# Second MLP's first weights decoded one unit per tile through a single buffer, and the token sums and splits moved from GpSimd to VectorE and spaced out

## The chip, the core and the metric

The kernel runs on one NeuronCore of a Trainium2 chip. TensorE (PE; its weight loads are shown as PEld), VectorE (DVE), ScalarE (ACT), GpSimd (POOL) and SyncE (SP, which here only issues DMAs) each work through a queue of their own in order, and wait for each other by semaphores. The metric is device time in microseconds, as a median over runs.

## What is computed

```python
def _moe_ref(x, w_in, w_out):            # first MLP
    h = x @ w_in
    g = h * (1.0 / (1.0 + np.exp(-1.702 * h)))
    return (g @ w_out).astype(np.float32)

def _moe2_ref(x, w_in, w_out):           # second MLP
    h = x @ w_in
    g = h * np.cos(h)
    return (g @ w_out).astype(np.float32)

# reference: attention of x (8 batches, 8 heads, 512 tokens, width 64) against 32 states,
# and of the states against x, gives 8 * (512 + 32) = 4608 rows of width 512;
# then _moe_ref and _moe2_ref over these rows (d_ff 2048), in float32
```

## The kernel before

Every float32 operand is split into a high part that TensorE takes exactly and a low rest, and a product is three matmuls (high-high, high-low, low-high). Weights come from HBM as 64-bit words of which a *unit* of 1024 columns is put together on chip: `top` and `bottom` on ScalarE, `bits` on VectorE, then `hi` (a copy on ScalarE) and `lo` (a subtraction on VectorE).

**First MLP.** Its steps are (t, c): token tile t (512 tokens; the tail, t = 8, has 256 rows of the states) and chunk c of 16 of the hidden width. The order of the tiles is 0 to 6, then the tail, then 7. In a step TensorE makes `hidden` (the tile `ph`) and then `second` of the step two before (into `py`). ScalarE and VectorE make the gate between them: `t` (ACT), `t` (DVE), `gh` (ACT), `gl` (DVE). For t = 1 to 7 the attention's values are folded into the weights: `sw_piece` makes them (POOL issues their store to DRAM, `sd<-swo`), and `load_sw` brings them back, 256 KB a step (`swt`), into a ring of eight tiles: that of step c + 8 is issued by SP at step c.

**The second MLP's weights on the way.** The second MLP multiplies 2x2 blocks with seven products where eight would be plain. For that each unit of its first weights becomes eight *leaves*: four blocks and four sums. `leaves` decodes a unit, splits the blocks (`hi(0)`, `lo`), makes four sums in place (`sums`), splits these (`hi(1)` on ACT, the subtraction on POOL), and stores both halves to DRAM (`ld<-leaf`, 1 MB each). All eight units are fetched and decoded in the steps of the tail and of tile 7, in the buffers of the first MLP's input weights as these come free. In tile 7 `prepare_first` also makes the seven sums and splits of the first pair of token tiles, with POOL for the arithmetic and ACT for the high parts.

**Second MLP.** A list of work is put in order by `Order`, a planner with a cost and a due time for each piece, that writes out one fixed order for each engine. A pair of token tiles has eight periods; a period is 15 blocks of six matmuls: seven products (`bankX`, `bankY`, `bankW`) and eight blocks of the second weights (`bankpy`, `bankF`). The first period has the seven products and the first MLP's last two `second` pieces. In periods 1 to 8 `unit` decodes the eight units of the second weights. `prepare` makes the sums and splits of the next pair of tokens: raw tiles loaded by SP (`raw<-yd`), sums and low parts on POOL, high parts on ACT, stores to DRAM (`od`). Its due times lie 8 us apart, but a piece may start as soon as its operands are there.

The planner's rule for the next piece, of those that could start first:

```python
at = {n: begin(n) for n in some}
first = min(at.values()) + 0.05
n = min((n for n in some if at[n] <= first), key=lambda n: (work[n][4], n))
```

Of the kernel before, what the change touches and what calls it, by code (L numbers as in the profile page):

```python
# [10 lines left out]
F32 = mybir.dt.float32  # L11
# [32 lines left out]
GROUP = 15 * BLOCK  # L44


class Order:
# [9 lines left out]
    def add(self, engine, cost, do, reads=(), writes=(), due=0.0, lag=0.0):  # L57
# [11 lines left out]
        self.work.append((engine, cost, do, tuple(after), due, lag))  # L69

    def write(self):
# [15 lines left out]
        def begin(n):  # L87
            return max(free[work[n][0]], max((ends[a] + SIGNAL for a in work[n][3]), default=0.0))

        while len(begun) < len(work):  # L90
# [11 lines left out]
            e, cost, _, _, _, lag = work[n]  # L102
# [15 lines left out]
def attention_two_mlps(  # L118
# [17 lines left out]
    xp = ctx.enter_context(tc.tile_pool(name="xp", bufs=2))  # L136
    ep = ctx.enter_context(tc.tile_pool(name="ep", bufs=2))
# [30 lines left out]
    def fetch_w(m, nm, j):  # L168

        src = {"i": (w_in1, w_in2), "o": (w_out1, w_out2)}[nm][m]  # L170
        place = 2 * j % (KF // 2) if m and nm == "i" else j
        raw = wp.tile([P, UNIT, 2], I32, name=f"raw{nm}{m}_{j}", tag=f"w{nm}{place}")
        for e in range(2):
            words = src[2 * j + e].bitcast(I32)
            if m and nm == "i":
                nc.sync.dma_start(
                    out=raw.rearrange("p (h e k f) w -> p h e k (f w)", h=2, e=2, k=2)[:, :, e, :, :],
                    in_=words.rearrange("p (h k f) -> p h k f", h=2, k=2),
                )
            elif nm == "i":  # L180
# [30 lines left out]
    def decode_end(entry=None):  # L211
# [3 lines left out]
        if entry is None and begun[0][0] == 1 and begun[0][1] == "i":  # L215
            return leaves()
# [19 lines left out]
    late = []  # L236

    def leaves():

        _, _, j, u, low = begun.pop(0)  # L240
        place = 2 * j % (KF // 2)
        ui = u.bitcast(I32)
        uq = u.rearrange("p (q f) -> p q f", q=4)
        out_ = []

        def bits():
            nc.vector.scalar_tensor_tensor(  # L247
                out=ui, in0=ui, scalar=3, in1=low, op0=ALU.logical_shift_left, op1=ALU.bitwise_or
            )

        def hi(n):
            out_.append(wp.tile([P, 4, 2, PAIR], F32R, name=f"leaf{j}_{n}", tag=f"wi{place + n}"))
            nc.scalar.activation(out=out_[n][:, :, 0, :], in_=uq, func=AF.Copy)

        def lo(n, engine):
# [12 lines left out]
        def lo_and_sums():  # L268
            lo(0, nc.vector)
            sums()  # L270
            late.append(lambda: (hi(1), lo(1, nc.gpsimd)))

        return bits, lambda: hi(0), lo_and_sums


# [905 lines left out]
```

## Time and profile before

| | us |
|---|---|
| median of 3 runs (1478.27 to 1480.67) | 1479.16 |
| the profiled execution | 1481.61 |
| its span, first to last instruction | 1479.8 |
| TensorE busy in the span | 1418.8 |
| VectorE busy | 961.4 |
| ScalarE busy | 735.1 |
| GpSimd busy | 228.2 |

The profiled execution is 2.45 us longer than the median of the runs, and 1.8 us of it lie outside the span. A matmul of 128x512 starts 0.227 us after the one before when nothing is waited for, so six of them, a block, take 1.36 us at the full clock. The granted clock is a share of 2.4 GHz: 1.00 is 2.4 GHz, and a stretch wholly at 0.50 is at 1.2 GHz.

### The profile page before, as it was taken

What the parts mean: (1) busy time and instruction counts of PE and PEld (TensorE: products, weight loads), DVE (VectorE), ACT (ScalarE), POOL (GpSimd) and SP (SyncE); (2) the same over time, 40 slices, a digit from 0 to 9 for tenths busy, and PEclk for the clock granted to TensorE, in tenths of its full rate; (3) what the DMA queues carried; (4) which work ended last, traced back from release to release, by engine and by line L of the source; (5) the groups of instructions that cost most, each with busy time, mean ns of one, the idle gap of its engine ahead of it and who ended that gap; (6) DMA issues with size and microseconds to landing.
All of it is one profiled execution on the core that took longest, in us unless ns stands there. A gap on an engine that the chain in (4) does not pass through costs nothing.

```text
span 1479.8 us, 19839 instructions
## 1 busy us (share of the span) xinstructions
PE 1418.8 (96%) x7134; PEld 1161.5 (78%) x7134; DVE 961.4 (65%) x1589; ACT 735.1 (50%) x1253; POOL 228.2 (15%) x222
## 2 busy tenths in 40 slices
PE   8999999999999999967889999899989999999998
PEld 5878888888878788956767787788878888888887
DVE  6875646565556555557568867766677677666664
ACT  6764343434443434445477545544455444544454
POOL 1111111101110001015625002500053000000000
PEclk9999999999999999978989999999999999999999
DMA  9756564656464443669677527853398236423253
GB/s 345 223 175 186 160 184 142 193 139 174 132 183 121 136 125 86 226 235 388 238 230 239 185 86 284 300 184 93 119 345 282 94 92 233 151 86 93 88 176 107
DMA packets 128226, 268.58 MB, mean 181 GB/s; under 512 B 17280, under 2 KB 35328, under 8 KB 126080
## 3 DMA queue, kind: packets, MB, share of 16 engines
q1 hardware_dynamic: 119024, 237.81, 48.5%
q0 software_dynamic: 8960, 29.37, 8.0%
q8 instruction: 57, 0.93, 0.3%
q14 instruction: 41, 0.34, 0.1%
q10 hardware_dynamic: 144, 0.13, 0.0%
HBM read 181.27 MB, written 85.98 MB: 181 GB/s over the span
## 4 chain that ended last, share of the span: by engine, by line
PE 82%; DVE 8%; DMA 4%; ACT 3%; issue 2%; POOL 1%; SPq 0%; ACTq 0%; DVEq 0%; POOLq 0%
PE py L540 22%; PE bankpy L704 12%; PE bankF L704 11%; PE bankX L694 10%; PE ph L485 10%; PE bankY L694 5%; PE psS L300 3%; PE bankW L694 3%; PE ph L493 2%; PE psA L359 1%; DMA rawi<-in_w_in 1%; DVE u L247 1%; DMA ws<-ld 1%; DVE r L676 1%; DVE leaf L256 1%
## 5 line engine op out<-in xcount | busy, mean ns | idle before, releaser
L540 PE MATMUL py<-gh,wo 128*128 128x512 f32 (+1 forms) x1152 | 369.4, 384 | 9.6 <-ACT gh L500 6.3
L540 PEld LDWEIGHTS py<-gh,wo 128*128 128x128 f32 x1152 | 217.7, 193 | 54.1 <-ACT gh L500 6.5
L704 PE MATMUL bankpy<-wo,g 128*128 128x512 f32 x864 | 221.6, 392 | 4.5 <-DVE g L684 3.3
L540 PE MATMUL py<-gl,wo 128*128 128x512 f32 (+1 forms) x576 | 221.3, 384 | 1.9 <-DVE gl L502 1.9
L500 ACT ACTIVATE gh<-t 128x512 fp32r<-128x512 f32 (+1 forms) x144 | 87.5, 608 | 262.0 <-DVE t L512 132.7
L502 DVE TENSOR_TENSOR gl<-t,gh 128x512 fp32r<-128x512 f32 (+1 forms) x144 | 104.1, 723 | 163.4 <-ACT gh L500 163.4
L704 PE MATMUL bankF<-wo,g 128*128 128x512 f32 x768 | 200.0, 395 | 9.8 <-DVE acc L844 6.5
L704 PEld LDWEIGHTS bankpy<-wo,g 128*128 128x128 f32 x864 | 162.0, 189 | 39.6 <-DVE g L684 4.7
L485 PE MATMUL ph<-xh,swt 128*128 128x512 f32 x448 | 163.6, 406 | 16.5 <-DVE t L512 16.5
L704 PEld LDWEIGHTS bankF<-wo,g 128*128 128x128 f32 x768 | 145.1, 190 | 43.5 <-DVE acc L844 7.4
L512 DVE SCALAR_TENSOR_TENSOR t<-t,ph 128x512 f32<-128x512 f32 (+1 forms) x144 | 94.0, 653 | 88.3 <-ACT t L510 88.0
L308 POOL DMA_DIRECT2D sd<-swo x112 | 66.9, 607 | 499.2 <-DVE swo L305 475.9
L844 DVE SCALAR_TENSOR_TENSOR acc<-bankF,acc 128x512 f32<-128x512 f32 x112 | 77.3, 690 | 98.4 <-PE bankF L704 94.3
L672 ACT ACTIVATE r<-C 128x512 f32<-128x512 f32 (+1 forms) x144 | 87.1, 605 | 96.1 <-DVE C L893 95.3
L540 PEld LDWEIGHTS py<-gl,wo 128*128 128x128 f32 x576 | 111.0, 193 | 23.9 <-DVE gl L502 3.4
L485 PEld LDWEIGHTS ph<-xh,swt 128*128 128x128 f32 x448 | 85.4, 191 | 46.3 <-DVE t L512 18.2
L510 ACT ACTIVATE t<-ph 128x512 f32<-128x512 f32 (+1 forms) x144 | 81.8, 568 | 74.3 <-PE ph L485 61.7
L678 ACT ACTIVATE r<-r 128x512 f32<-128x512 f32 (+1 forms) x144 | 84.6, 603 | 61.6 <-DVE r L676 61.4
L676 DVE TENSOR_TENSOR r<-r,n 128x512 f32<-128x512 f32 (+1 forms) x144 | 107.4, 760 | 2.7
L684 DVE TENSOR_TENSOR g<-r,g 128x512 fp32r<-128x512 f32 (+1 forms) x144 | 94.8, 688 | 22.1 <-ACT g L682 21.4
L887 ACT ACTIVATE C<-bankX 128x512 f32<-128x512 f32 x96 | 57.1, 595 | 102.7 <-PE bankX L694 102.5
L680 DVE TENSOR_TENSOR r<-r,C 128x512 f32<-128x512 f32 (+1 forms) x144 | 96.8, 701 | 10.4 <-ACT r L678 10.1
(147 smaller groups left out, 2151.0 us busy)
## 6 DMA issues: line engine op xcount, KB each, us to landing
ws<-ld SPq DMA_DIRECT2D x256, 256.0 KB, 2.9
sd<-swo POOLq DMA_DIRECT2D x112, 256.0 KB, 3.9
swt<-sd SPq DMA_DIRECT2D x112, 256.0 KB, 4.1
rawi<-in_w_in SPq DMA_DIRECT2D x32, 512.0 KB, 7.6
rawo<-in_w_out SPq DMA_DIRECT2D x32, 512.0 KB, 7.2
ld<-leaf SPq DMA_DIRECT2D x16, 1024.0 KB, 4.9
xT_t<-in_xT SPq DMA_DIRECT2D x36, 256.0 KB, 4.3
xN_t<-in_xN SPq DMA_DIRECT2D x16, 512.0 KB, 4.4
```

Source lines behind the costliest of these rows:

```text
L485: nc.tensor.matmul(ph, l, r, start=(g == 0 and i == 0), stop=(g == 1 and i == 2))
L500: nc.scalar.activation(out=gh, in_=g, func=AF.Copy)
L502: return lambda: nc.vector.tensor_tensor(out=gl, in0=g, in1=gh.bitcast(F32), op=ALU.subtract)
L512: nc.vector.scalar_tensor_tensor(out=g, in0=t1, scalar=1.0, in1=ph, op0=ALU.add, op1=ALU.mult)
L540: nc.tensor.matmul(yt[k], l, r, start=(c == 0 and i == 0), stop=(c == KF - 1 and i == 2))
L672: add("ACT", 0.62 * u, lambda: nc.scalar.activation(out=R(), in_=C(), func=AF.Copy, bias=0.25), [ck], [rk], due - 5)
L676: add("DVE", 0.69 * u, lambda: nc.vector.tensor_tensor(out=R(), in0=R(), in1=N(), op=ALU.subtract), [nk], [rk], due - 3.6)
L678: add("ACT", 0.73 * u, lambda: nc.scalar.activation(out=R(), in_=R(), func=AF.Sin, scale=TURN), [], [rk], due - 2.7)
L680: add("DVE", 0.69 * u, lambda: nc.vector.tensor_tensor(out=R(), in0=R(), in1=C(), op=ALU.mult), [ck], [rk], due - 1.8)
L684: add("DVE", 0.69 * u, lambda: nc.vector.tensor_tensor(out=G(1), in0=R(), in1=G(0).bitcast(F32), op=ALU.subtract), [rk, ("g", g, 0)], [("g ...
L694: nc.tensor.matmul(b, w[:, wl, k, :], y[:, yl, :], start=i in (0, 1, 5) and n == 0, stop=i in (3, 5, 6) and n == 5, skip_group_check=True)
L704: nc.tensor.matmul(bank(at_), l, r, start=start and i == 0, stop=stop and i == 2, skip_group_check=True)
```

## The change

- A new pool `xq` with one buffer a tag takes over the tags xh2, xl2, xh3, xl3. The ring of `swt` has four tiles and not eight; `load_sw` for step c + 4 is issued at step c. The space that is saved is one tile of 8 KB a partition, the tag `eight`.
- `leaves` becomes `leaf_unit`. Units 0 to 5 go through `eight`, one in each of tiles 1 to 6: fetched at step 4 of the tile, decoded at steps 8 and 9, split at 12 and 13, summed at 15, and the sums split at steps 0 and 1 of the next tile. Units 6 and 7 go through first weights' buffers around the tail, from its steps 2 and 6. All subtractions are on VectorE.
- Units 0 to 3 of the second weights (`UNITS_AHEAD`) are decoded in tile 7, at steps 7, 9, 11 and 13; the planner has units 4 to 7.
- `prepare_first`, `prepare` and `prepare_tail` use VectorE for all sums and low parts. `prepare_first` starts a step earlier.
- A piece of work can have an earliest time (`early`) in the planner. `prepare` spreads its loads, splits and sums over the whole of seven periods with it, loads 8 us ahead.
- In the second MLP two of the six tiles `C` and two of the raw tiles lie in `eight` (`more`).

TensorE's instructions and their order are the same in both kernels.

```diff
-def add(self, engine, cost, do, reads=(), writes=(), due=0.0, lag=0.0):
+def add(self, engine, cost, do, reads=(), writes=(), due=0.0, lag=0.0, early=0.0):
...
-            return max(free[work[n][0]], max((ends[a] + SIGNAL ...), default=0.0))
+            return max(free[work[n][0]], work[n][6], max((ends[a] + SIGNAL ...), default=0.0))
...
+    def leaf_unit(j):
+        spare = j < KF // 2 - 2
+        def place(n, shape, dtype, name):
+            if spare:
+                return xq.tile(shape, dtype, name=name, tag="eight")
+            return wp.tile(shape, dtype, name=name, tag=f"wi{2 * (j % 2) + n}")
...
+        def lo(n):
+            w = st["leaf"]
+            nc.vector.tensor_tensor(out=w[:, :, 1, :], in0=quarters(), in1=w[:, :, 0, :].bitcast(F32), op=ALU.subtract)
+            nc.sync.dma_start(
...
-            late.append(lambda: (hi(1), lo(1, nc.gpsimd)))
...
-        t = xp.tile([P, 2, 2, P], F32R, name="swt", tag=("xh2", "xl2", "xh3", "xl3")[i])
+            t = xq.tile([P, 2, 2, P], F32R, name="swt", tag=("xh2", "xl2", "xh3", "xl3")[c % 4])
...
-                nc.gpsimd.tensor_tensor(out=lo, in0=first_raw[a, k], in1=hi.bitcast(F32), op=ALU.subtract)
+                nc.vector.tensor_tensor(out=lo, in0=first_raw[a, k], in1=hi.bitcast(F32), op=ALU.subtract)
...
+            start = when(8 * (p - 1) + (p == 1))
+            step = (when(8 * p - 1) - start - 16) / 14
...
-                        when(8 * (p - 1)) + 8 * n, 3.0)
+                        start + step * n - 6, 4.0, start + step * n - 8)
...
-                        add("POOL", 1.3, lambda s=s, h=h, A=A: nc.gpsimd.tensor_tensor(
+                        add("DVE", 0.69, lambda s=s, h=h, A=A: nc.vector.tensor_tensor(
...
-                for u in range(G):
+                for u in range(UNITS_AHEAD, G):
...
+            if j < B - 2:
+                s = steps1.index((0, j + 1, 0))
+                plan_ = (4, fetch), (8, top), (9, bottom), (9, bits), (12, partial(hi, 0)), (13, partial(lo, 0)), \
+                    (15, sums), (16, partial(hi, 1)), (17, partial(lo, 1))
+            else:
+                s = steps1.index((0, B, 2 + 4 * (j - B + 2)))
+                plan_ = (0, fetch), (4, top), (4, bottom), (5, bits), (5, partial(hi, 0)), (5, partial(lo, 0)), \
+                    (6, sums), (6, partial(hi, 1)), (7, partial(lo, 1))
...
+        for j in range(UNITS_AHEAD):
+            units[last_t, 2 * j + 7] = (1, "o", j)
...
-            if t == 1 and c < 4 or 1 < t < B and c + 8 < KF:
-                load_sw(t, c + 8)
+            if t == 1 and 4 <= c < KF - 4 or 1 < t < B and c + 4 < KF:
+                load_sw(t, c + 4)
```

Three places in the built order of the engines' queues. The first is ScalarE at the end of the tail and the start of tile 7 in the kernel before (`t` and `gh` are the gate, `u` and `rawi` top and bottom of a unit, `leaf` its high parts, the number behind `rawi` or `leaf` the unit's buffer):

```order
L253 ACTIVATE leaf_0_6161<-u 128x4x256
L510 ACTIVATE t_6196<-ph 128x256
L204 ACTIVATE u<-rawi_2_6043 128x1024
L500 ACTIVATE gh<-t_6196 128x256
L207 ACTIVATE rawi_2_6043<-rawi_2_6043 128x1024
L253 ACTIVATE leaf_1_6208<-u 128x4x256
L510 ACTIVATE t_6237<-ph 128x256
L500 ACTIVATE gh<-t_6237 128x256
L253 ACTIVATE leaf_0_6244<-u 128x4x256
L510 ACTIVATE t_6276<-ph 128x512
L204 ACTIVATE u<-rawi_3_6205 128x1024
```

And the same queue in the tail in the changed kernel:

```order
L249 ACTIVATE u<-rawi_6_5849 128x1024
L255 ACTIVATE rawi_6_5849<-rawi_6_5849 128x1024
L523 ACTIVATE t_6030<-ph 128x256
L513 ACTIVATE gh<-t_6030 128x256
L268 ACTIVATE leaf_0_6038<-u 128x4x256
L523 ACTIVATE t_6067<-ph 128x256
L513 ACTIVATE gh<-t_6067 128x256
L268 ACTIVATE leaf_1_6078<-u 128x4x256
L523 ACTIVATE t_6105<-ph 128x256
L513 ACTIVATE gh<-t_6105 128x256
L523 ACTIVATE t_6139<-ph 128x256
```

Before, nearly every step has pieces of two units between its gates; now one unit has four steps to itself, and steps without a unit follow.

The second place is SyncE's queue around the turn from tile 4 to tile 5, before (`yd` stores the first MLP's rows, `xN_t` and `xT_t` are attention inputs):

```order
L317 DMA swt<-sd_1_101 128x512 x3
L344 DMA xT_t<-in_xT 128x512 x2
L317 DMA swt<-sd_2_102 128x512
L547 DMA yd_116<-o 128x512 x4
L344 DMA xT_t<-in_xT 128x512 x2
L325 DMA sblk<-in_stT 128x256
L317 DMA swt<-sd_2_102 128x512 x3
```

And there now:

```order
L273 DMA ld_134<-leaf_0_4047 128x2048
L330 DMA swt<-sd_0_103 128x512 x3
L357 DMA xT_t<-in_xT 128x512 x2
L330 DMA swt<-sd_1_104 128x512
L560 DMA yd_119<-o 128x512 x4
L357 DMA xT_t<-in_xT 128x512 x2
L338 DMA sblk<-in_stT 128x256
L273 DMA ld_134<-leaf_1_4233 128x2048
L330 DMA swt<-sd_1_104 128x512 x3
L362 DMA xN_t<-in_xN 128x4x256
L242 DMA rawi_4_4438<-in_w_in 128x2x512 x2
L330 DMA swt<-sd_2_105 128x512
```

Two leaf stores and a fetch of two pieces have come in between the loads of `swt`, and these are of steps nearer by.

The third place is the start of the second pair of tokens in the second MLP (period 8). Before, POOL has there (L759 low parts, L766 sums):

```order
L759 TENSOR_TENSOR y_a_6649<-raw,y_a_6649 128x512
L766 TENSOR_TENSOR raw<-raw 128x512
L759 TENSOR_TENSOR y_a_6388<-raw,y_a_6388 128x512
L766 TENSOR_TENSOR raw<-raw 128x512
L759 TENSOR_TENSOR y_a_6649<-raw,y_a_6649 128x512
```

Now VectorE has, among its own work (L776 low parts, L783 sums):

```order
L861 SCALAR_TENSOR_TENSOR acc_7222<-bankF,acc_7222 128x512
L691 TENSOR_TENSOR r<-r,n 128x512
L695 TENSOR_TENSOR r<-r,C 128x512 x2
L776 TENSOR_TENSOR y_a_6396<-raw,y_a_6396 128x512
L695 TENSOR_TENSOR r<-r,more 128x512
L699 TENSOR_TENSOR g_7032<-r,g_7032 128x512
L699 TENSOR_TENSOR g_7119<-r,g_7118 128x512
L699 TENSOR_TENSOR g_7081<-r,g_7080 128x512
L776 TENSOR_TENSOR y_a_6396<-more,y_a_6396 128x512
L910 TENSOR_TENSOR C<-bankY,C 128x512
```

The pieces that stood one behind the other on POOL stand single among VectorE's.

## Rows read from the trace of the kernel before

**Rows 1.** The page: busy us, share, instructions; clock in 40 slices.
```profile
PE 1418.8 (96%) x7134; PEld 1161.5 (78%) x7134; DVE 961.4 (65%) x1589; ACT 735.1 (50%) x1253; POOL 228.2 (15%) x222
...
PEclk9999999999999999978989999999999999999999
```

**Rows 2.** Windows by stage: length, busy us of each engine, clock, DMA share, GB/s.
```profile
140.00:582.90 442.90, 442.86 (x2555) 358.26 (x2554) 257.07 (x522) 179.10 (x325) 49.97 (x84) 1.00 0.53 149
582.90:739.20 156.30, 129.59 (x687) 110.71 (x686) 90.93 (x115) 74.29 (x121) 59.69 (x37) 0.90 0.73 261
739.20:832.40 93.20, 82.22 (x337) 65.20 (x336) 72.09 (x92) 71.71 (x108) 32.40 (x22) 0.95 0.72 236
832.40:914.00 81.60, 81.60 (x361) 67.57 (x360) 57.31 (x91) 37.60 (x65) 4.44 (x3) 1.00 0.46 156
914.00:962.40 48.40, 43.46 (x182) 34.65 (x181) 39.03 (x47) 29.07 (x53) 27.18 (x20) 0.96 0.86 298
...
1084.80:1132.20 47.40, 43.38 (x181) 34.64 (x180) 38.81 (x47) 29.18 (x53) 27.14 (x20) 0.96 0.88 303
```

**Rows 3.** The chain, in order of time: start us, us, piece (tail, then tile 7).
```profile
592.79 1.43 PE ph L493 x12
594.23 1.44 PE py L540 x12
...
724.36 2.72 PE py L540 x12
727.08 1.36 PE ph L485 x6
```

**Rows 4.** Timeline of ACT in the tail: start, us, idle before and releaser.
```profile
635.82 1.12 ACT L204 ACTIVATE u<-rawi 128x1024 f32<-128x1024 f32 x1 [9.71 <-DMA rawi<-in_w_in]
```

**Rows 5.** Timeline of PE: the tail, and tile 7.
```profile
637.30 0.58 PE L540 MATMUL py<-gh,wo 128*128 128x256 f32 x1 [6.28 <-ACT gh L500]
...
683.90 0.79 PE L485 MATMUL ph<-xh,swt 128*128 128x512 f32 x1 [3.79 <-DVE t L512]
```

**Rows 6.** Timeline of DVE: a unit alone, and one beside POOL.
```profile
610.92 1.22 DVE L247 SCALAR_TENSOR_TENSOR u<-u,rawi 128x1024 int32<-128x1024 int32 x1
...
614.58 0.42 DVE L263 TENSOR_TENSOR u<-u 128x256 f32<-128x256 f32 x1
...
639.85 2.90 DVE L247 SCALAR_TENSOR_TENSOR u<-u,rawi 128x1024 int32<-128x1024 int32 x1
```

**Rows 7.** Timeline of POOL there.
```profile
639.29 2.37 POOL L256 TENSOR_TENSOR leaf<-u,leaf 128x1024 fp32r<-128x1024 f32 x1 [18.62 <-ACT leaf L253]
```

**Rows 8.** DVE by line, 962.4 to 1084.8: count, busy us, mean ns, idle before.
```profile
L676 DVE TENSOR_TENSOR r<-r,n 128x512 f32<-128x512 f32 x23 | 16.5, 736 | 0.4
```

**Rows 9.** DVE by line, 1084.8 to 1132.2.
```profile
L676 DVE TENSOR_TENSOR r<-r,n 128x512 f32<-128x512 f32 x10 | 13.0, 1307 | 0.2
```

**Rows 10.** The first two periods of the second MLP as windows.
```profile
739.20:759.90 20.70, 15.09 (x68) 12.18 (x66) 11.29 (x14) 16.55 (x23) 4.20 (x3) 0.95 0.71 235
759.90:786.50 26.60, 24.91 (x91) 19.67 (x92) 19.01 (x25) 19.70 (x33) 9.81 (x7) 0.84 0.67 218
```

**Rows 11.** Timeline of ACT in the first period, and in period 8.
```profile
758.11 1.24 ACT L546 ACTIVATE o<-py 128x512 f32<-128x512 f32 x2 [3.06 <-DMA yd<-o]
...
935.84 0.63 ACT L757 ACTIVATE y_a<-raw 128x512 fp32r<-128x512 f32 x1 [5.89 <-DMA raw<-yd]
```

**Rows 12.** Timeline of PE behind these two.
```profile
759.88 2.93 PE L694 MATMUL bankX<-y_a,ws 128*128 128x512 f32 x6 [5.61 <-ACT C L887]
...
938.75 2.83 PE L704 MATMUL bankF<-wo,g 128*128 128x512 f32 x6 [3.73 <-DVE acc L844]
```

**Rows 13.** DMA issues: queue, count, KB each, median us from issue to landing.
```profile
swt<-sd SPq DMA_DIRECT2D x112, 256.0 KB, 4.1
rawi<-in_w_in SPq DMA_DIRECT2D x32, 512.0 KB, 7.6
...
ld<-leaf SPq DMA_DIRECT2D x16, 1024.0 KB, 4.9
```

More of the change, by code (lines that the diff above doesn't have):

```diff
@@ L68, in add @@
         after.discard(n)
-        self.work.append((engine, cost, do, tuple(after), due, lag))
+        self.work.append((engine, cost, do, tuple(after), due, lag, early))
     def write(self):
@@ L101, in write @@
             at, n = best
-            e, cost, _, _, _, lag = work[n]
+            e, cost, _, _, _, lag, _ = work[n]
             free[e] = at + cost
@@ L170, in fetch_w @@
         src = {"i": (w_in1, w_in2), "o": (w_out1, w_out2)}[nm][m]
-        place = 2 * j % (KF // 2) if m and nm == "i" else j
-        raw = wp.tile([P, UNIT, 2], I32, name=f"raw{nm}{m}_{j}", tag=f"w{nm}{place}")
+        raw = wp.tile([P, UNIT, 2], I32, name=f"raw{nm}{m}_{j}", tag=f"w{nm}{j}")
         for e in range(2):
             words = src[2 * j + e].bitcast(I32)
[L175 to L180, printed above, removed]
+            if nm == "i":
                 nc.sync.dma_start(
@@ L234, in decode_end, with fetch, top, bottom @@
         return bits, hi, lo
[L236 to L244, printed above, removed]
+    def leaf_unit(j):
+        spare = j < KF // 2 - 2
+        st = {}
+        def place(n, shape, dtype, name):
+            if spare:
+                return xq.tile(shape, dtype, name=name, tag="eight")
+            return wp.tile(shape, dtype, name=name, tag=f"wi{2 * (j % 2) + n}")
+        def fetch():
+            st["raw"] = place(0, [P, UNIT, 2], I32, f"rawi1_{j}")
+            for e in range(2):
+                nc.sync.dma_start(
+                    out=st["raw"].rearrange("p (h e k f) w -> p h e k (f w)", h=2, e=2, k=2)[:, :, e, :, :],
+                    in_=w_in2[2 * j + e].bitcast(I32).rearrange("p (h k f) -> p h k f", h=2, k=2),
+                )
+        def top():
+            st["u"] = wtp.tile([P, UNIT], F32, name="u", tag="u")
+            nc.scalar.activation(
+                out=st["u"], in_=st["raw"][:, :, 1].bitcast(F32), func=AF.Prelu, scale=2.0**-112, alpha=-(2.0**32)
+            )
+        def bottom():
+            low = st["raw"][:, :, 0]
+            nc.scalar.activation(out=low, in_=low.bitcast(U32), func=AF.Copy, scale=TOP3)
@@ L246, in bits, with quarters @@
         def bits():
+            ui = st["u"].bitcast(I32)
             nc.vector.scalar_tensor_tensor(
-                out=ui, in0=ui, scalar=3, in1=low, op0=ALU.logical_shift_left, op1=ALU.bitwise_or
+                out=ui, in0=ui, scalar=3, in1=st["raw"][:, :, 0], op0=ALU.logical_shift_left, op1=ALU.bitwise_or
             )
+        def quarters():
+            return st["u"].rearrange("p (q f) -> p q f", q=4)
         def hi(n):
-            out_.append(wp.tile([P, 4, 2, PAIR], F32R, name=f"leaf{j}_{n}", tag=f"wi{place + n}"))
@@ L266, in sums @@
             nc.vector.tensor_tensor(out=b21, in0=b21, in1=b22, op=ALU.subtract)
[L268 to L273 removed]
+        return fetch, top, bottom, bits, hi, lo, sums
     xtile = {}
```

74 lines of the change are left out of this document (36 added, 38 removed).

## The prediction

> **What bounds the kernel now.** I read the page first. TensorE is busy for 1418.8 of 1479.8 us and its clock falls below nine tenths of full only between about 630 and 780 us [rows 1]. So TensorE is the bound nearly everywhere, and what can be won is where it waits or runs at the lower clock. The windows by stage say where that is [rows 2]. From 140 to 583 us (tiles 1 to 6) it is busy for 442.86 of 442.90 us, from 832 to 914 us for all 81.6. The second of these holds four periods, so a period takes 20.4 us when nothing is late. Four stretches are worse: tail and tile 7 (582.9 to 739.2), the first four periods (739.2 to 832.4), the two periods in which the second pair's tokens are prepared (914.0 to 962.4), and the like two for the third pair (1084.8 to 1132.2). POOL is busy in just these four.
>
> What each of them costs is its length less the work in it. A tail step is 1.43 + 1.44 us, a step of tile 7 is 1.36 + 2.72 us, and two more `second` pieces of 2.72 us run over into the tail's first steps, while the tail's last two run over into tile 7 [rows 3]. So the first stretch holds 16 x 2.87 (45.9), 16 x 1.36 (21.8), 16 x 2.72 (43.5), and two small weight pieces of half a tail piece each (1.4): 112.6 us. It takes 156.3: **43.7 us too long**. The first four periods hold 7 x 1.36 + 2 x 2.72 (15.0) and 3 x 20.4 (61.2), 76.2 us, and take 93.2: **17.0 too long**. The two others hold 40.8 each and take 48.4 and 47.4: **7.6 and 6.6 too long**. Together 74.9 us. The rest of the excess, at the kernel's start and end, the change does not touch.
>
> Two causes show in the rows. One is queues that stand still in order. In the tail ScalarE waits 9.71 us for a unit's fetch [rows 4], and the gate behind it holds TensorE up for 6.28 us; in tile 7 TensorE waits 3.79 us for VectorE's `t` [rows 5], which stands behind a whole unit. The other is POOL. The same VectorE operation takes 1.22 us alone and 2.90 us [rows 6] when POOL's 2.37 us subtraction [rows 7] runs beside it. In the quiet second MLP a 512-wide subtraction takes 736 ns, while the tokens are prepared 1307 ns [rows 8, 9].
>
> **The change, part by part.** TensorE's order is untouched, so only waits and clock can move.
>
> Tail and tile 7. Six of eight unit decodes leave. The two that stay are the tail's (fetched at steps 2 and 6), with `t` now ahead of the sums in VectorE's queue and no POOL beside them. Up to 628 us the kernel before ran two units there and TensorE lost next to nothing; its first long wait is that of 637.30 [rows 5]. I leave 1 us for these. Tile 7 gets new work: 22 sums and low parts on VectorE, at 0.74 us by [rows 8] 16.3 us, and four decodes of two 1024-wide operations at 1.22 us [rows 6], 9.8 us. Its own two gate operations take 1.4 us a step, 22 us in 16 steps. That is 48 us in 65.3. The fullest steps are 8 and 10: 1.4 + 1.5 + 2.4 = 5.3 us against 4.08, and the steps between them have 2.9, so the queue is behind by 1.2 us at most, where `second` runs two steps (8.2 us) after `hidden`. I leave 1.7 us for waits on landings. So 43.7 goes to 2.7: **41 us gained**; bounds 25 (see the rivals) and 43.
>
> First four periods. The wait at 759.88 is of another kind: ScalarE's third store of the first MLP's last rows waits for the first one's landing [rows 11], and TensorE waits 5.61 us for an eviction behind it [rows 12]. The stores, the two buffers and the fetch ahead of them in SP's queue stand as before. So the 5.7 us of period 0 (20.7 less 15.0 [rows 10]) stay, and with them about 2.5 us at the lower clock just behind (the window of 26.6 us has 0.84, and so the clock takes 4.3 us of it, and I put the larger part to that wait). The rest of the 17.0, 8.8 us, comes while POOL prepares tokens and eight units are decoded. Four units are decoded earlier now and POOL is out. I leave 0.8: **8 gained**, bounds 3 and 17.
>
> Second and third pair. 14.2 us. Both causes are there: the stretched operations, and ScalarE standing 5.89 us at a split for a reload of `raw` [rows 11], which made TensorE wait 3.73 us for VectorE's `acc` [rows 12]. Now each reload is planned 8 us ahead of its split and the splits lie 9 us apart. On VectorE 22 operations of 0.74 us come on 7 periods: 2.3 us a period on 14.3 (57.31 over four [rows 2]), of 20.4. I leave 1.2: **13 gained**, bounds 6 and 14.
>
> Tiles 1 to 6. A unit adds to VectorE one `bits` at 1.22 us, two `lo` of the same size and four sums at 0.42 us [rows 6]: 5.3 us on a tile's 73.8 us, where it is busy for 58% [rows 2]. Its pieces stand in steps of their own, none beside another. Their cover is VectorE's slack; without it a unit would cost 5.3 us and six units 32. Their DMAs: a fetch of two pieces (7.6 us to land) and two stores (4.9 us) a tile [rows 13]. Behind each in SP's queue stand loads of `swt`, now four steps ahead: 4 x 4.08 = 16.3 us less 4.1 us of landing leaves 12 us. Nothing in the order makes SP wait for that long: the fetch comes three steps after the store whose buffer it takes. I take 1 us, bounds 0 and 8. The tail's tokens (two low parts) move for nothing.
>
> Sum: 41 + 8 + 13 - 1 = **61 us**. From the profiled execution's 1481.6 that is 1420.6; the runs' median lies 2.45 us lower, so **1418 us**.
>
> **A rule to weigh.** VectorE is already the second busiest engine (65% [rows 1]), and the change moves work onto it. The Trainium skill, Perfetto Trace Analysis, "Optimizing Scalar/DVE Operations", says that with a saturated VectorE some of its work may go to ScalarE or even GpSimd, which would speak against this change; it adds that GpSimd and VectorE share a read port, so that such a move may not help. By the first half the first of the rivals below, at 1440 us, would be the likely case; the rows on POOL bear out the second half (2.90 against 1.22 us), so I keep to the sum.
>
> **The rivals.** *Tile 7 stays crowded.* Steps 7 to 14 have a decode in every second step and token work in most, across two in-order queues that wait for each other. If each of the four decodes made TensorE wait as the units did (3.79 us [rows 5]) and lose about 1.7 us to the clock, 22 us stay there: 1440. For it speaks that this was the mechanism before, and that the first tokens' raw tiles (and then the leaves of the first period) land late in the same steps; against it that those steps had four sums, two low parts and stretched operations at once, about twice as much. 16%.
>
> *The opening wait goes too.* If the store's landing is faster with fewer transfers about, 5.7 + 2.5 us more: 1410. The transfer ahead of it is the same 1 MB fetch, which speaks against. 14%.
>
> *The planner spaces only on paper.* `early` is a time in the planner, and the engines start when their waits end. If the pieces bunch up behind a late landing, the 13 us of the later pairs are not won: 1431. Against it: in the built order they stand singly among VectorE's other work, and a queue keeps its order. 7%.
>
> *Slower: the short ring.* If SP stands at a fetch for the buffer `eight` while `swt` loads queue behind it, TensorE waits for whatever is beyond the 12 us of lead. To end above the time before, that must eat 61 us, so 10 us in each of six tiles, a stand of over 22 us at each fetch. The leaf store that it waits for was issued 12 us before and lands in 4.9. 3%.
>
> **How the numbers follow.** My forecast, 1409 to 1428 with 1418 the likeliest, gets 59%, the crowded tile 16% (1430 to 1450), the opening 14% (1404 to 1413), the paper spacing 7%, slower 3%, and 1% is left for no change. The low end of the range is 1406 (the opening's 1410 and a little less left over elsewhere), the high end 1438: two in ten or fewer lie outside, most of them crowded tiles. A measurement of this kernel tells 0.2%, about 3 us, from no change. All cases but the last two are faster by far more: 96% faster, 1% same, 3% slower.
>
> **What would show it.** Right: the stretch from the tail's first step to the first product takes 114 to 118 us, with no step of VectorE over its plain time; the two windows of 48.4 and 47.4 us come near 41; POOL is busy only with store issues and the tail's split; the first period still has a wait of over 5 us for an eviction behind a store. Wrong: TensorE waits for `t` or `gl` in tile 7, TensorE waits for `swt` in tiles 1 to 6, or the wait of period 0 is gone.

## The result, and the profile after

The changed kernel takes **1425.34 us** (median of 4 runs, 1424.54 to 1427.49) against 1479.35 us (1478.27 to 1480.67) of the kernel before, runs of the same chip: a ratio of 0.9637 (0.9620 to 0.9653), so 54 us faster. The forecast was 1418, with a range of 1406 to 1438. The profiled execution has a span of 1423.3 us, 56.5 less than before.

The first line of the page answers to [rows 1]: most of POOL's work has left (66.8 of the 72.6 us that stay are the issuing of the stores `sd<-swo`), VectorE's share has risen, and TensorE's is at 98%.

```profile
PE 1397.0 (98%) x7134; PEld 1149.0 (81%) x7134; DVE 965.6 (68%) x1687; ACT 733.3 (52%) x1253; POOL 72.6 (5%) x124
```

The windows answer to [rows 2, 10]. Columns: window in us from the span's start, its length, then busy time of TensorE, its weight loads, VectorE, ScalarE and POOL with instruction counts, granted clock, DMA share, GB/s. They are tiles 1 to 6, tail with tile 7, the second MLP's first and second period, and the two periods in which the second and the third pair's tokens are prepared.

```profile
125.80:587.30 461.50, 457.91 (x2622) 368.40 (x2620) 290.81 (x568) 206.87 (x359) 50.62 (x86) 1.00 0.62 186
587.30:706.50 119.20, 114.61 (x686) 101.93 (x685) 71.71 (x114) 62.66 (x109) 4.03 (x7) 1.00 0.58 197
706.50:725.90 19.40, 15.80 (x68) 12.10 (x67) 14.05 (x17) 17.74 (x25) 0.00 (x0) 1.00 0.63 219
725.90:749.30 23.40, 22.53 (x90) 17.99 (x91) 19.39 (x32) 17.67 (x30) 0.00 (x0) 0.93 0.64 223
871.70:912.50 40.80, 40.80 (x181) 33.78 (x180) 30.92 (x52) 24.42 (x44) 0.00 (x0) 1.00 0.69 237
1034.90:1075.70 40.80, 40.80 (x181) 33.78 (x180) 30.76 (x52) 24.58 (x44) 0.00 (x0) 1.00 0.67 235
```

With the work that the prediction counted, the stretches read so:

| stretch | work, us | too long before | too long after | gain | forecast |
|---|---|---|---|---|---|
| tail and tile 7 | 112.6 | 43.7 | 6.7 | 37.0 | 41 |
| first four periods | 76.2 | 17.0 | 7.4 | 9.6 | 8 |
| second and third pair | 81.6 | 14.2 | 0.0 | 14.2 | 13 |
| tiles 1 to 6 | | | | -4.4 | -1 |
| sum | | | | 56.4 | 61 |

The row of tiles 1 to 6 is counted from the start of the span, so that the rows add up. From tile 1's own start these tiles lose 4.9 us: 461.5 us now against 456.6 us in the kernel before, whose window is

```profile
126.30:582.90 456.60, 456.56 (x2621) 368.78 (x2620) 263.23 (x531) 185.45 (x336) 50.68 (x86) 1.00 0.54 150
```

The first four periods are 706.55 to 790.11, the third and fourth of them 20.4 each. In tile 7 every step from 653.5 on takes 4.08 us, with no wait. What is left stands in three places. In the tail and in tiles 1 to 6 TensorE waits for VectorE, and VectorE or ScalarE has a piece of a weights' unit ahead. In the timelines a row is start, length, engine and line, operation, out<-in, and in brackets the idle time before it and what ended it. Line 453 is the transposes of the attention, 506 a tail step's `hidden`, 523 and 525 the gate's two halves of `t`, 268 a unit's `hi`, 272 its `lo`, 259 its `bits`, 282 the last of its sums. TensorE's timeline of the changed kernel:

```profile
178.60 0.63 PE L453 MATMUL psB<-ident,a 128*128 128x128 f32 x4 [0.71 <-DVE a L448]
...
625.67 1.70 PE L506 MATMUL ph<-xtail,wi 128*128 128x256 f32 x12 [1.15 <-DVE t L525]
636.28 1.70 PE L506 MATMUL ph<-xtail,wi 128*128 128x256 f32 x12 [1.72 <-DVE t L525]
640.78 1.46 PE L506 MATMUL ph<-xtail,wi 128*128 128x256 f32 x10 [1.37 <-DVE t L525]
```

ScalarE's timeline of it, in the tail:

```profile
623.83 1.06 ACT L268 ACTIVATE leaf<-u 128x1024 fp32r<-128x1024 f32 x1 [2.21 <-DVE u L282]
624.80 0.37 ACT L523 ACTIVATE t<-ph 128x256 f32<-128x256 f32 x1
...
633.58 1.06 ACT L268 ACTIVATE leaf<-u 128x1024 fp32r<-128x1024 f32 x1 [1.69 <-DVE u L259]
```

VectorE's, in tile 1 and in the tail:

```profile
174.40 1.23 DVE L259 SCALAR_TENSOR_TENSOR u<-u,rawi 128x1024 int32<-128x1024 int32 x1 [0.34 <-ACT rawi L255]
...
625.20 0.42 DVE L525 SCALAR_TENSOR_TENSOR t<-t,ph 128x256 f32<-128x256 f32 x1 [1.40 <-ACT t L523]
...
634.67 1.22 DVE L272 TENSOR_TENSOR leaf<-u,leaf 128x1024 fp32r<-128x1024 f32 x1 [1.18 <-ACT leaf L268]
```

In the tail, ScalarE stands 2.21 us at a `hi` whose sums VectorE is still working on. The next step's `t` comes behind it, and TensorE waits for that `t`: so with the waits at 625.67 and 640.78. The longest, 1.72 us at 636.28, has another piece ahead: the `hi` of 633.58 stands 1.69 us for `bits`, VectorE's `lo` waits for that `hi`, and VectorE's `t` comes behind the `lo`. In tiles 1 to 6 the transposes' wait stands in five of the six tiles; in each, the 1.23 us `bits` runs ahead of the normalization on line 448.

The last place is the end of the first period. Line 709 is a product, 904 its eviction on ScalarE, 559 the eviction of a store. TensorE's timeline there:

```profile
725.86 2.93 PE L709 MATMUL bankX<-y_a,ws 128*128 128x512 f32 x6 [3.19 <-ACT C L904]
```

And ScalarE's:

```profile
724.11 1.21 ACT L559 ACTIVATE o<-py 128x512 f32<-128x512 f32 x2 [0.15 <-DMA yd<-o]
725.22 0.59 ACT L904 ACTIVATE C<-bankX 128x512 f32<-128x512 f32 x1
```

This is the wait of [rows 11, 12], but ScalarE now waits only 0.15 us for the landing, having been busy for 17.74 of the period's 19.4 us.

### The profile page after: what moved, and what is told of

It is laid out like the page before. It is cut to its first block, busy times and chain, and to the rows that moved or that the text cites. A ratio compares the mean times of both kernels' runs of the same rounds, so it can differ in the third digit from the quotient of the medians.

```text
span 1423.3 us, 19770 instructions
## 1 busy us (share of the span) xinstructions
PE 1397.0 (98%) x7134; PEld 1149.0 (81%) x7134; DVE 965.6 (68%) x1687; ACT 733.3 (52%) x1253; POOL 72.6 (5%) x124
## 4 chain that ended last, share of the span: by engine, by line
PE 85%; DVE 7%; ACT 4%; issue 2%; DMA 1%; SPq 0%; POOL 0%; ACTq 0%; DVEq 0%
PE py L553 20%; PE bankpy L719 14%; PE bankF L719 12%; PE bankX L709 12%; PE ph L498 9%; PE bankY L709 6%; PE bankW L709 3%; PE psS L307 3%; PE ph L506 3%; DVE t L525 1%; PE psA L372 1%; ACT gh L513 1%; DVE u L215 1%; DVE xs L473 1%; PE psC L462 1%
## 5 line engine op out<-in xcount | busy, mean ns | idle before, releaser
L553 PE MATMUL py<-gh,wo 128*128 128x512 f32 (+1 forms) x1152 | 362.4, 378 | 2.1 <-ACT wo L221 1.2
L553 PEld LDWEIGHTS py<-gh,wo 128*128 128x128 f32 x1152 | 213.0, 188 | 44.2 <-DVE wo L225 2.4
L553 PE MATMUL py<-gl,wo 128*128 128x512 f32 (+1 forms) x576 | 217.4, 377 | 0.0
L515 DVE TENSOR_TENSOR gl<-t,gh 128x512 fp32r<-128x512 f32 (+1 forms) x144 | 97.4, 676 | 144.4 <-ACT gh L513 144.4
L719 PE MATMUL bankF<-wo,g 128*128 128x512 f32 x768 | 195.0, 389 | 0.0
L699 DVE TENSOR_TENSOR g<-r,g 128x512 fp32r<-128x512 f32 (+1 forms) x144 | 91.5, 658 | 22.4 <-ACT g L697 22.3
L687 ACT ACTIVATE r<-C 128x512 f32<-128x512 f32 (+1 forms) x96 | 58.4, 608 | 73.1 <-DVE C L910 72.5
L691 DVE TENSOR_TENSOR r<-r,n 128x512 f32<-128x512 f32 (+1 forms) x144 | 92.8, 659 | 2.0
L315 POOL DMA_DIRECT2D sd<-swo x112 | 66.8, 605 | 504.2 <-DVE swo L312 463.5
L697 ACT ACTIVATE g<-r 128x512 fp32r<-128x512 f32 (+1 forms) x144 | 82.8, 602 | 18.1 <-DVE r L695 18.0
L709 PE MATMUL bankX<-y_a,ws 128*128 128x512 f32 x336 | 86.8, 394 | 3.6 <-ACT C L904 3.2
```

Source lines behind the costliest of these rows:

```text
L515: return lambda: nc.vector.tensor_tensor(out=gl, in0=g, in1=gh.bitcast(F32), op=ALU.subtract)
L553: nc.tensor.matmul(yt[k], l, r, start=(c == 0 and i == 0), stop=(c == KF - 1 and i == 2))
L691: add("DVE", 0.69 * u, lambda: nc.vector.tensor_tensor(out=R(), in0=R(), in1=N(), op=ALU.subtract), [nk], [rk], due - 3.6)
L697: add("ACT", 0.62 * u, lambda: nc.scalar.activation(out=G(0), in_=R(), func=AF.Copy), [rk], [("g", g, 0)], due - 0.9)
L699: add("DVE", 0.69 * u, lambda: nc.vector.tensor_tensor(out=G(1), in0=R(), in1=G(0).bitcast(F32), op=ALU.subtract), [rk, ("g", g, 0)], [("g ...
L709: nc.tensor.matmul(b, w[:, wl, k, :], y[:, yl, :], start=i in (0, 1, 5) and n == 0, stop=i in (3, 5, 6) and n == 5, skip_group_check=True)
```

## The experiments

All times below are medians, to be held against 1425.3 (the changed kernel) or 1479.4 to 1480.6 (the kernel before, run beside them). Tile 1 starts between 125.6 and 128.9 us in these profiled executions, whatever was edited. So stretches are compared, each from its own start. The changed kernel was not run again beside these experiments. The kernel before was, and its medians lie 1.2 us apart, while single runs of one kernel lie up to 4.9 us apart: a difference of 2 us between medians says little without the stretch that it comes from.

**1. The units' move alone.** The new buffers and the short ring stay; everything else of the change is undone:

```diff
-UNITS_AHEAD = 4
+UNITS_AHEAD = 0
 # sums and splits of tokens, all pairs and the tail:
-nc.vector.tensor_tensor(...)   # add("DVE", 0.69, ...)
+nc.gpsimd.tensor_tensor(...)   # add("POOL", 1.3, ...)
 # their loads, splits and sums: the old due times, no earliest time
```

> Only the decode of the second MLP's first weights is changed; the sums and splits of tokens are on POOL at their old times again, and all eight units of the second weights are decoded in the second MLP. Theory (the units' move is the tail's and tile 7's gain of 37 us; the engine and the spread are the gain of the pairs, 14.2, and most of the opening's 9.6): tail and tile 7 take 120 to 130 us, the two windows of the pairs 47 to 48 us again, time about 1453 us. Rival (tile 7 was long because POOL prepares the first tokens there): tile 7 alone stays 15 us or more too long, time about 1468 us.

1445.76 us (1445.56 to 1448.42), ratio 0.9773 (0.9758 to 0.9787). Tail and tile 7 take 119.3 us, as in the whole change, though POOL prepares the first tokens in tile 7. The first four periods are 14.8 us too long, the pairs 13.4. Its windows, in the columns of above: tail and tile 7, and the two pairs.

```profile
589.80:709.10 119.30, 114.72 (x687) 102.02 (x687) 53.34 (x86) 51.71 (x98) 33.74 (x29) 1.00 0.59 201
...
881.70:928.00 46.30, 42.52 (x182) 33.31 (x181) 38.98 (x47) 29.07 (x53) 27.12 (x20) 1.00 0.90 310
1050.40:1099.10 48.70, 44.43 (x182) 35.50 (x181) 39.06 (x48) 28.93 (x53) 26.66 (x20) 0.93 0.88 301
```

So the move of the units is the whole gain of the largest stretch. It fell better than either theory's number: without second weights' units in its steps, tile 7 did not mind POOL, and 2.2 of the opening's 9.6 us are here already.

**2. POOL's part in that stretch, from the other side.** The kernel before, all its units where they were, with the units' second low part and the first pair's sums and splits on VectorE:

```diff
-            late.append(lambda: (hi(1), lo(1, nc.gpsimd)))
+            late.append(lambda: (hi(1), lo(1, nc.vector)))
 # prepare_first: nc.gpsimd -> nc.vector, twice
```

> The kernel before, with its order and all its units in tail and tile 7, but the units' second low part and the first pair's sums and splits on VectorE instead of POOL; the later pairs stay on POOL. Theory (tail and tile 7 are too long because queues stand in order at late units; POOL beside VectorE adds little): that stretch still holds 35 us or more of its 43.7 us of excess, time 1470 to 1482 us. Rival (the stretched VectorE steps, 21.8 us in that stretch, are the cause): the excess falls to 22 us or less, time about 1457 us.

1473.01 us (1472.41 to 1474.09), ratio 0.9948 (0.9930 to 0.9966). `bits` are back at 1218 ns, where they have a mean of 1855 ns before. The kernel before by line, 582 to 733 us (count, busy us, mean ns, idle before):

```profile
L247 DVE SCALAR_TENSOR_TENSOR u<-u,rawi 128x1024 int32<-128x1024 int32 x8 | 14.8, 1855 | 0.0
```

The experiment by line, the same stretch:

```profile
L247 DVE SCALAR_TENSOR_TENSOR u<-u,rawi 128x1024 int32<-128x1024 int32 x8 | 9.7, 1218 | 0.0
```

And its window of tail and tile 7:

```profile
582.60:732.40 149.80, 125.84 (x687) 107.51 (x686) 92.40 (x145) 73.88 (x121) 4.02 (x7) 0.93 0.76 272
```

The stretch takes 149.8 us instead of 156.3: 37.2 of the 43.7 us stay. Against the plain step of their line and shape, VectorE's steps in that stretch took some 22 us more before. Here 2.0 us are left, all in one step beside the tail's split, which stays on POOL. So 20 us less of stretching, with the moved steps now on VectorE, gave TensorE 6.5 us. The 37.2 us that stay go with the late units: run 1, which moves them, has 6.7.

**3. The pairs: engine or spread?** The changed kernel, once with the sums and splits of tokens on POOL at the new times, once on VectorE at the old times:

```diff
 # tokens_pool: the five tensor_tensor of tokens
-add("DVE", 0.69, lambda ...: nc.vector.tensor_tensor(
+add("POOL", 1.3, lambda ...: nc.gpsimd.tensor_tensor(
```

```diff
 # no_spread
-                        start + step * n - 6, 4.0, start + step * n - 8)
+                        when(8 * (p - 1)) + 8 * n, 3.0)
-                    due = start + step * n + 12
+                    due = when(8 * (p - 1)) + 8 * n + 12
-                            ... [A], [k0, (s, h)], due, 0.0, due - 12)
+                            ... [A], [k0, (s, h)], due)
```

> The changed kernel with the sums and splits of tokens on POOL again, at the new, spread times. Theory (a VectorE step beside a POOL step is held up, and this made the pairs long): each window of a pair is 4 to 7 us longer than 40.8, VectorE's 512-wide subtraction again has a mean over 1000 ns there, time about 1443 us. Rival (the reloads that came late made the pairs long, and the spread cured it): the windows stay within 1.5 us of 40.8, time about 1428 us, whatever the engine.

> The changed kernel with the old due times of the tokens' loads, sums and splits, and no earliest times; all on VectorE. Theory (the engine is the larger part): the windows of the pairs are 1 to 4 us longer than 40.8, by ScalarE's wait for a reload as in the kernel before, time about 1430 us. Rival (the spread is the larger part): the windows are 5 to 7 us longer, time about 1438 us.

1427.36 us (1426.54 to 1428.81) and 1426.40 us (1426.02 to 1427.43). **The theory of each falls**, and so does the second's rival; the first's rival has the windows and the time right, but the second run shows that the spread is not needed. In either kernel the two windows are 40.8 us, not a tenth too long. The windows of the one on POOL:

```profile
874.80:915.60 40.80, 40.80 (x182) 33.78 (x181) 29.53 (x42) 24.74 (x44) 12.87 (x9) 1.00 0.71 237
1038.00:1078.80 40.80, 40.80 (x182) 33.78 (x181) 30.04 (x42) 24.85 (x44) 12.62 (x9) 1.00 0.69 234
```

Those of the one without spread:

```profile
872.70:913.50 40.80, 40.80 (x182) 33.79 (x181) 34.63 (x59) 27.00 (x49) 0.00 (x0) 1.00 0.84 288
1035.90:1076.70 40.80, 40.80 (x182) 33.78 (x181) 34.78 (x59) 27.08 (x49) 0.00 (x0) 1.00 0.84 289
```

In the pairs only the two together, POOL at the old times, cost something (run 1; that it has no second weights' units in tile 7 either does not matter here, since TensorE waits nowhere in the pairs of units0, below). The first four periods tell the same: 6.4 and 8.6 us too long, near the changed kernel's 7.4, where run 1 has 14.8. Tile 7 differs: with the tokens on POOL and four units decoded there, tail and tile 7 take 121.0 us, some 1.8 more than in the whole change or in run 1, and TensorE waits twice for VectorE's `gl`. Each part alone is free there, both together are not:

```profile
589.60:710.60 121.00, 115.49 (x686) 101.69 (x685) 66.17 (x92) 62.07 (x109) 35.57 (x29) 1.00 0.56 194
```

What costs in the pairs must be a thing that each of the edits takes away. In run 1 it shows in ScalarE's timeline: line 774 is the split of a raw tile, and it waits for the tile's reload.

```profile
901.32 0.63 ACT L774 ACTIVATE y_a<-raw 128x512 fp32r<-128x512 f32 x1 [3.75 <-DMA raw<-yd]
...
1071.53 0.63 ACT L774 ACTIVATE y_s<-raw 128x512 fp32r<-128x512 f32 x1 [5.25 <-DMA raw<-yd]
```

With the tokens on POOL at the new times ScalarE's longest wait for a reload is 0.7 us, without spread 1.1. TensorE's longest wait in run 1's pairs comes 3 us behind the second of these:

```profile
1074.45 2.93 PE L719 MATMUL bankF<-wo,g 128*128 128x512 f32 x6 [3.04 <-DVE acc L861]
```

**4. A number in the planner.** The raw tile's last reader is a POOL step, which the planner takes for 1.3 us; in a period of run 1 the splits' POOL steps take 1.27 to 1.40 us and the sums 1.33 to 1.74, one behind the other. A reload of `raw` lands after 4.6 us (median in the second pair's window, 3.9 to 6.5), where the planner has 3.0. If the planner runs ahead of the engines, it puts ScalarE's split, and all that stands behind it, too early in the order. So run 1 again, with one number changed in each:

```diff
 # pool_cost, both steps of prepare()
-                        add("POOL", 1.3, ...
+                        add("POOL", 2.0, ...
```

```diff
 # reload_lag: the planner's time for a reload to land
-                        when(8 * (p - 1)) + 8 * n, 3.0)
+                        when(8 * (p - 1)) + 8 * n, 6.0)
```

> The kernel with the weights' units alone moved (tokens on POOL at the old times), with the planner's cost of a POOL step at 2.0 instead of 1.3 us. Theory (the planner takes POOL for faster than it runs, so ScalarE stands in order at splits whose reload is not there): the pairs' excess of 13.4 us falls below 5, time about 1437 us. Rival (POOL's rate and the stretched VectorE steps themselves): 1444 to 1448 us.

> The same kernel with the planner's time for a reload to land at 6.0 instead of 3.0 us. Theory (a reload takes 5 to 6 us there, ScalarE's split is ordered for 3): ScalarE's waits for raw go, the pairs' excess falls from 13.4 to 5 us or less, time about 1437 us. Rival (the reload is issued late because POOL frees its buffer late, by whatever plan): 1444 to 1448 us.

1431.17 us (1431.15 to 1431.70) and 1439.77 us (1438.86 to 1443.75), against run 1's 1445.76. The work and its engines are the same; only the order differs. With POOL's cost at 2.0 the pairs are 1.4 us too long instead of 13.4, and the first four periods 12.1 instead of 14.8. The windows of the pairs:

```profile
876.40:917.90 41.50, 41.26 (x181) 33.61 (x180) 33.45 (x43) 26.18 (x48) 23.39 (x18) 1.00 0.90 326
1040.30:1081.80 41.50, 41.26 (x181) 33.63 (x180) 33.94 (x43) 26.29 (x48) 23.59 (x18) 1.00 0.90 316
```

ScalarE's longest wait for a reload there is 0.68 us, by its timeline:

```profile
1064.77 0.63 ACT L774 ACTIVATE y_s<-raw 128x512 fp32r<-128x512 f32 x1 [0.68 <-DMA raw<-yd]
```

VectorE is still held up by POOL there: line 691 takes 1144 ns in the second of these windows, 686 ns in the changed kernel's. By line, with POOL's cost at 2.0:

```profile
L691 DVE TENSOR_TENSOR r<-r,n 128x512 f32<-128x512 f32 x9 | 10.2, 1144 | 0.1
```

And in the changed kernel, third pair:

```profile
L691 DVE TENSOR_TENSOR r<-r,n 128x512 f32<-128x512 f32 x7 | 4.8, 686 | 0.0
```

TensorE hardly feels it. So another order alone, with engines and work unchanged, takes the pairs' loss away, and with it goes ScalarE's stand at a split planned too early. The longer landing alone leaves 5.6 us, a little more than its theory allowed, so it cures the larger half; waits of 2.2 and 1.2 us for reloads stay there. In the first four periods the planner's number wins only 2.7 us. That 2.0 is above what POOL's steps take says that it gives room, not that it is the right number; which other cost of the plan is short was not followed.

**5. The opening.** Units of the second weights decoded in tile 7 or not; the last four units held back; the third and fourth store's eviction given a later due time:

```diff
 # units0
-UNITS_AHEAD = 4
+UNITS_AHEAD = 0
 # units_late: no unit before about the third period
-            add("ACT", 1.15, top, [w], [u, "tops"], due - 5)
+            add("ACT", 1.15, top, [w], [u, "tops"], due - 5, 0.0, due - 60)
 # stores_late
-                        [f"py{k}"], [("o", o)], when(0, 8), 2.5)
+                        [f"py{k}"], [("o", o)], when(0, 8 + 2 * k), 2.5)
```

> The changed kernel with none of the second weights' units decoded in tile 7: all eight are decoded in the second MLP, as before. Theory (the opening's gain of 9.6 us is for the most part that four decodes left it): the first three periods hold 5 to 10 us more excess, tile 7 stays at 4.08 us a step, time about 1432 us. Rival (POOL's leaving is the opening's gain): the opening is within 2 us of the changed kernel's, time about 1426 us.

> The changed kernel with the last four units of the second weights held back to the third period and later. Theory (ScalarE is full in the opening, 17.7 of 19.4 us, and the eviction for which TensorE waits stands behind a unit's pieces): the 3.6 us gap at the end of the first period goes to under 1, the opening's excess from 7.4 to 3 or less, time about 1421 us. Rival (the third store's wait for the first one's landing sets it, as the prediction had it): the gap stays above 3 us, with ScalarE idle for over 2 us before that store, time about 1425 us.

> The changed kernel with the last two evictions of the first MLP's rows given later due times, so that ScalarE empties the bank for which TensorE waits ahead of them. By both theories of the opening's wait (full ScalarE, or the store's landing) the 3.6 us gap falls to under 1.5 us and the time to about 1421 us; by a third (the period's wait is handed on to the py banks that these stores free) the second period starts earlier and is as much longer, time about 1425 us.

1426.46 us (1426.02 to 1427.13): the first theory falls, and the rival's number holds. The opening is 7.6 us too long without four units ahead, 7.4 with them. But the wait is another: without them it is TensorE's 5.6 us of the kernel before again, with ScalarE idle for a landing. The rows of units0, ScalarE's and TensorE's:

```profile
726.04 0.60 ACT L559 ACTIVATE o<-py 128x512 f32<-128x512 f32 x1 [3.13 <-DMA yd<-o]
...
728.04 2.93 PE L709 MATMUL bankX<-y_a,ws 128*128 128x512 f32 x6 [5.60 <-ACT C L904]
```

1425.06 us (1423.56 to 1427.57): the rival holds in time and wait, at the fourth store and not the third. With the units gone, ScalarE is idle for 3.46 us there, since the second store's landing frees its buffer, and TensorE waits 4.37 us at one place, where the changed kernel has 0.42 and 3.19 us at two. ScalarE's timeline of it, and TensorE's wait:

```profile
721.78 0.58 ACT L559 ACTIVATE o<-py 128x512 f32<-128x512 f32 x1
725.83 0.60 ACT L559 ACTIVATE o<-py 128x512 f32<-128x512 f32 x1 [3.46 <-DMA yd<-o]
726.32 0.59 ACT L904 ACTIVATE C<-bankX 128x512 f32<-128x512 f32 x1
...
726.97 2.92 PE L709 MATMUL bankX<-y_a,ws 128*128 128x512 f32 x6 [4.37 <-ACT C L904]
```

1423.42 us (1423.04 to 1426.18) with the stores later: the opening is 5.4 us too long, between its theories. Waits of 0.44 and 1.83 us stay, the longer one with units' pieces ahead of the eviction:

```profile
727.68 1.66 PE L709 MATMUL bankX<-y_a,ws 128*128 128x512 f32 x6 [1.83 <-ACT C L904]
```

So two causes lie over each other, a full ScalarE and the landing; taking one leaves much of the wait to the other.

**6. The two waits in the first MLP.**

```diff
 # bits_later
-                plan_ = (4, fetch), (8, top), (9, bottom), (9, bits), ...
+                plan_ = (4, fetch), (8, top), (9, bottom), (11, bits), ...
 # tail_sparse
-                plan_ = (0, fetch), (4, top), (4, bottom), (5, bits), (5, hi 0), (5, lo 0), (6, sums), (6, hi 1), (7, lo 1)
+                plan_ = (0, fetch), (3, top), (4, bottom), (5, bits), (6, hi 0), (7, lo 0), (8, sums), (9, hi 1), (10, lo 1)
```

> The changed kernel with a unit's bits in tiles 1 to 6 two steps later. Theory (bits stand on VectorE ahead of the attention's second normalization, for which TensorE's transposes wait 0.7 us each in five tiles): first step of the tail 3.5 to 4.4 us earlier, time about 1421 us. Rival (the extra VectorE and ScalarE work of a unit costs that, wherever it stands): the start of the tail within 1 us, time about 1425 us.

> The changed kernel with the tail's two units spread over ten steps each, so that no step of a unit stands on ScalarE behind one of VectorE in the same step. Theory (in the tail TensorE waits because the next step's t on ScalarE stands behind a leaf that waits for the sums or bits on VectorE): the three waits of 1.4 to 2.0 us in the tail go, tail and tile 7 take 114 to 116 us instead of 119.25, time about 1421 us. Rival (the tail's steps of 2.87 us are simply too full): the waits come back elsewhere in the tail or in tile 7, time within 1 us of 1425.

1423.88 us (1421.31 to 1425.27) with later `bits`, between theory and rival. Tiles 1 to 6 take 459.4 us, 2.1 less than after: five tiles gain about 0.7 us each, and tile 5, whose attention pieces lie at other steps, gets a wait of its own, as TensorE's timeline shows:

```profile
497.89 0.63 PE L453 MATMUL psB<-ident,a 128*128 128x128 f32 x4 [1.18 <-DVE a L448]
```

1428.91 us (1424.83 to 1429.36) with the tail spread, not faster, and neither theory's time: the three waits in the tail are gone, and tile 7 has one of 4.22 us. Waits that come back elsewhere were the rival's sign, but not because the steps are full. The last leaf's store had moved to tile 7's first step, and in SP's queue the loads of the first tokens stand behind it. SP's timeline, four leaf stores over 20.94 us, then the loads:

```profile
624.45 20.94 SPq L273 DMA_DIRECT2D ld<-leaf  x4
...
646.02 1.89 SPq L581 DMA_DIRECT2D yraw_xN<-yd  x2
```

ScalarE waits for those tokens, with tile 7's `t` behind it in its queue:

```profile
655.66 0.63 ACT L605 ACTIVATE y_a<-yraw_xs 128x512 fp32r<-128x512 f32 x1 [7.99 <-DMA yraw_xs<-yd]
```

The expectation had counted ScalarE and VectorE, not the store that moved with the piece.

**7. All four places at once.** As above, but the last `lo` in the tail's last step, the first tokens one step later, and `bits` left where they were in tile 5:

```diff
+                plan_ = (0, fetch), (3, top), (3, bottom), (4, bits), (5, hi 0), (6, lo 0), (7, sums), (8, hi 1), (9, lo 1)
+            first_pair[last_t, 2 + n] = part
+                ... (9, bottom), (9 if j + 1 == STATE_0 else 11, bits), ...
 # with units_late and stores_late
```

> The changed kernel with four edits together: the tail's units spread over nine steps with the last leaf stored before tile 7 (and the first tokens' preparation one step later), a unit's bits two steps later in all tiles but the one of the state's own scores, the last four units of the second weights held back, and the last two evictions of the first MLP's rows due after the bank that TensorE waits for. Theory (each of the four waits is a place in an in-order queue, and in the opening two of them lie over each other so that each edit alone shows little): 3.4 us in tiles 1 to 6, 5 in the tail, 5 to 6 in the opening, time about 1411 us. Rival (the waits are handed on, as with the tail's spread alone): two or more of the three come back, time 1417 us or more.

**1411.65 us** (1410.86 to 1412.64), ratio to before 0.9542 (0.9529 to 0.9555), where the changed kernel has 0.9620 to 0.9653. It beats both, by 68 and 14 us. Tiles 1 to 6 win 3.2 us, the tail 5.0, the opening 5.4. Its windows, tiles 1 to 6, tail and tile 7, first and second period:

```profile
126.00:584.30 458.30, 457.99 (x2622) 368.42 (x2620) 289.95 (x568) 206.72 (x359) 50.72 (x86) 1.00 0.62 187
584.30:698.50 114.20, 113.84 (x686) 101.76 (x685) 71.73 (x115) 64.03 (x110) 4.01 (x7) 1.00 0.61 205
698.50:714.30 15.80, 15.12 (x67) 12.20 (x65) 7.12 (x12) 8.09 (x13) 0.00 (x0) 1.00 0.67 214
714.30:735.90 21.60, 21.11 (x91) 16.85 (x92) 16.63 (x30) 14.59 (x27) 0.00 (x0) 1.00 0.72 259
```

The two edits of the opening that gave 0.6 and 2.0 us apart give 5.4 together, and the clock no longer falls in the second period (1.00 where after has 0.93).

## Why the prediction was right, and where it was not

The stretches gave 56.4 us for 61, partly by luck: two of them fell 7.4 us short together, and two came out 2.8 us better. The rest of the 7 us between 1418 and 1425.3 lies in the 2.45 us taken off because the profiled execution of the kernel before was longer than its median; that of the changed kernel is 0.3 us shorter than its own. Of its signs, 114 to 118 us for tail and tile 7 came as 119.2, and one step of VectorE was over its plain time (2.66 for 0.69 us, beside the tail's split on POOL). None of its three signs of being wrong came.

- **Tail and tile 7, 41 forecast, 37.0 measured.** The mechanism held: run 1 gets all of it by the units' move alone. Tile 7's new load, sized at a backlog of 1.2 us at most, costs nothing, and "tile 7 stays crowded" is out. The term that was mis-sized is the 1 us for the two units left in the tail. It rested on the kernel before losing next to nothing up to 628 us. But there the second halves of a unit came a step later; in the changed plan `hi` stands on ScalarE behind sums or `bits` of the same step on VectorE, and that costs 4.2 us by the three waits, 5.0 by run 7. The order of the changed kernel shows it; the prediction looked at VectorE's queue and not at ScalarE's.
- **First four periods, 8 forecast, 9.6 measured.** Right in size, with the reason half right. The store's landing still holds the period (run 5), but ScalarE's own load had grown to reach the same moment, which the prediction did not have: its sign, an eviction over 5 us late behind a store, came as 3.19 us, with 0.15 us of it the landing. "Four units are decoded earlier" shortened that wait and brought nothing in sum. What did bring the gain is shown in part only. The units' move alone leaves 14.8 of the 17.0 us, and with the tokens moved and spread as well, as in units0, 7.6 are left. Of these 7.2 us the planner's number wins 2.7; how the other 4.5 divide among stretched steps, POOL's rate and other numbers of the plan stays open.
- **Second and third pair, 13 forecast, 14.2 measured.** Right in size, but of the two causes named one cost next to nothing. ScalarE's stand at the reload was the cost. The stretched VectorE steps cost under 1.4 us (run 4). The rival "spaces only on paper" is out, though not because the spacing is needed: the change cures this twice over.
- **Tiles 1 to 6, -1 forecast, -4.4 measured**, inside its bounds of 0 to 8. "None beside another" held among the unit's own pieces; the attention's normalization, which stands behind them and the gate's two steps in VectorE's queue, was not looked at. Run 7 gets 3.2 us of it back; of the other 1.7 from tile 1's own start no experiment shows the cause. The short ring never made TensorE wait for `swt`; its loads land in 5.0 us, 4.1 before [rows 13].
- **The cause POOL** was given more weight than it has: 6.5 us in tail and tile 7 (run 2), at most 1.4 in the pairs, an open part of 4.5 in the opening. Some 20 us of stretched steps less are not 20 us of TensorE. The Trainium skill, Perfetto Trace Analysis, "Optimizing Scalar/DVE Operations", says that moving work between VectorE and GpSimd may not help since they share a read port. Run 3 agrees where the tokens are spread: on POOL or on VectorE they give medians 2.0 us apart, with ranges that overlap. At the old times the move did help, 1445.76 us in run 1 against 1426.40 without spread, and by run 4 a later place in the order gives 14.6 of these 19.4 us without any move.

## What to carry over

A stretched or slow step costs only where a wait ends with it: before moving work to another engine, see whether the loss is a stand in an in-order queue, because then a later place in the order (here one number of the planner) may cure it. When two causes end at the same moment, each edit alone shows little; try them together before dropping either. And when a piece is moved, move its store in mind too: what stands behind it on the queue that issues it may be the next stage's load.

## What the runs showed of the hardware

- A VectorE step with two SBUF inputs that meets a POOL step can take far longer: `bits` 2.90 us for 1.22 [rows 6], a mean of 1855 against 1218 ns in the stretch. POOL's own 512-wide steps took 1.27 to 1.74 us in the period of run 1 that was read. The Trainium skill, SBUF — State Buffer, "Who interferes with whom", has the rule that a VectorE instruction with two SBUF inputs contends with a GpSimd one that reads SBUF. The rows agree.
- At the end of the first period, a wait of TensorE of 3.19 us (the changed kernel) or 4.37 us (units_late) was followed by a lower granted clock in the second, 0.93 and 0.90. One of 2.79 us (the tokens on POOL, run 3), 1.83 us (stores_late) or 0.69 us (the last kernel) was not: 1.00 in each.
